# The third-last tile stored in one transfer instead of 16, and a new order for the last tile

## The chip, the cores and the metric

The kernel runs on one core of one Trainium2 chip. The metric is the device time of one execution in microseconds (us), as a median of several runs. One profiled execution of each kernel gives a trace; its span is about 1.8 us shorter than the device time of the same execution (1034.08 us against 1035.88 for the kernel before). Single executions of one kernel differ by up to 3 us. So wherever a few tenths matter I compare a piece of the trace that doesn't carry this scatter, called **the tail**: the time from the start of the last 512-column matmul (the last gate projection) to the end of the span. It is 8.38 us in the kernel before.

## The reference

Attention over spatially reduced keys and values, then a feed-forward block with a rectified gate:

```python
kv_pool = kv.reshape(B, H // r, r, W // r, r, C).mean(axis=(2, 4))
k = v = kv_pool.reshape(B, -1, C) @ w_sr
x = softmax(q @ k.T / sqrt(C)) @ v           # 49152 tokens of 128 features
out = (maximum(x @ w_gate, 0) * (x @ w_val)) @ w_out   # inner width 1536, float32 out
```

## The kernel before

The tokens are worked in 96 tiles of 512. A tile passes through stages that are software-pipelined: while tile k is attended to, tile k-3 runs its value and gate projections in 12 steps and tile k-4 its output projection. Each value/gate step writes one 128x512 block of `hT`. The output projection sums 12 blocks. It comes in two forms:

```python
def out_proj(k, fb):
    if k == NT - 2:                      # token-major: hT is the weight, 4 x 128 columns
        if fb == 0:
            o_banks[k] = bank([128, NS, 128])
        for s in range(NS):
            out_add(k, fb, s, o_banks[k][:, s, :], fb == 0 and s == 0)
        return
    if fb == 0:                          # feature-major: one matmul of 512 columns
        o_banks[k] = bank([128, T])
    nc.tensor.matmul(o_banks[k], wo16[:, fb, :], hTs[k][:, fb, :], ...)

def out_turn(k):                         # after a feature-major tile
    nc.vector.transpose(o_t, o_banks.pop(k))
    nc.gpsimd.tensor_scalar(o_sb..., o_t..., 1.0 / X_SCALE**2, None, op0=ALU.mult)
    ...                                  # in the first and last group of 4 tiles: 16 pieces of 16 KB
    return moves

def out_last(k):                         # tile 95: slices 0 and 1, then 2, then 3
    o_ps = bank([128, 2, 128])
    for s in range(2):
        for fb in range(NFB - 1):
            out_add(k, fb, s, o_ps[:, s], fb == 0 and s == 0)
    for s in range(2):
        out_add(k, NFB - 1, s, o_ps[:, s], False)
    out_scale(k, nc.vector, slice(0, 2), o_ps)
    out_store(k, slice(0, 2))
    for s in range(2, NS):
        o_ps = bank([128, 1, 128])
        for fb in range(NFB):
            out_add(k, fb, s, o_ps[:, 0], fb == 0)
        out_scale(k, (nc.scalar, nc.vector)[s % 2], slice(s, s + 1), o_ps)
    out_store(k, slice(2, NS))
...
# in the loop over stages: out_moves are issued two a step, in steps 2 to 9 of the next stage
    if step == NFB - 1 and k < last:
        out_moves = out_turn(kO)
    if 2 <= step < 10:
        for _ in range(2):
            if out_moves:
                nc.sync.dma_start(*out_moves.pop())
```

All stores are issued by SyncE, which works through its instructions in order. A token-major tile lies in the order of the output rows and goes out in one transfer of 128 packets of 2 KB, one from each partition.

The softmax here doesn't subtract the row's maximum and nothing guards it: scores larger than these inputs give would overflow.

## Time and profile before

| | before |
|---|---|
| device time | 1035.74 us median of 3 runs (1035.46 to 1036.62) |
| TensorE busy | 1023.5 us, 99% of the span |
| tail: last 512-column matmul at 1025.70, span's end at 1034.08 | 8.38 us |
| SyncE issuing pieces and stores, with one pause of 0.4 us at 1020.9 | 1013.2 to 1030.8 us |
| last store issued | 1030.44 us |

A line of the timeline reads: start, duration, engine, line of the kernel, operation, what it writes and reads, how many; in brackets, how long the engine sat idle before and who released it. A row "SPq" is SyncE issuing a transfer; its duration is the issuing, not the moving of data. The prediction below shows the lines that matter.

### The profile page before, as it was taken

How to read it: one execution, taken by the hardware profiler on the slowest of the kernel's cores; microseconds unless marked ns; L12 is line 12 of the kernel's file. 1: busy time of each engine (PE TensorE's matmuls, PEld its weight loads, DVE VectorE, ACT ScalarE, POOL GpSimd, SP SyncE). 2: the span in 40 equal slices, each digit the busy share in tenths (PEclk: the TensorE clock that was granted, in tenths of full speed). 3: DMA queues.
4: the chain of work that ended last, by engine and by line, in shares of the span. 5: the costliest groups of instructions: out<-in, count | busy, mean ns of one | idle time of the engine just before them, and what ended most of it. 6: DMA issues, size and time to landing. Idle time of an engine off the chain costs nothing.

```text
span 1034.1 us, 19981 instructions
## 1 busy us (share of the span) xinstructions
PE 1023.5 (99%) x6540; PEld 543.3 (53%) x6540; DVE 910.6 (88%) x1669; ACT 909.6 (88%) x1749; POOL 281.4 (27%) x288
## 2 busy tenths in 40 slices
PE   8999999999999999999999999999999999999998
PEld 5555555555555555555555555555555555555554
DVE  3888889998989898998889898989898989888897
ACT  4988899888888889888888888888898888889986
POOL 1212146521211125642212121664121211111111
PEclk9999999999999999999999999999999999999999
DMA  8936396562543547736345157573652533513122
GB/s 292 133 57 74 84 198 144 83 92 43 82 67 50 80 120 161 169 53 89 55 64 88 31 86 151 142 161 57 82 78 42 78 60 56 86 31 67 31 46 48
DMA packets 330840, 93.34 MB, mean 90 GB/s; under 512 B 310768, under 2 KB 324080, under 8 KB 330736
## 3 DMA queue, kind: packets, MB, share of 16 engines
q1 hardware_dynamic: 315648, 78.76, 39.1%
q0 software_dynamic: 14944, 13.24, 10.6%
q8 instruction: 51, 0.84, 0.3%
q14 instruction: 53, 0.43, 0.2%
q10 hardware_dynamic: 144, 0.07, 0.0%
HBM read 53.94 MB, written 26.35 MB: 78 GB/s over the span
## 4 chain that ended last, share of the span: by engine, by line
PE 97%; DMA 2%; DVE 0%; SPq 0%; ACT 0%; issue 0%
PE bank_ps L278 24%; PE bank_ps L289 24%; PE bank_ps L313 24%; PE bank_ps L240 12%; PE bank_ps L229 12%; DMA parts<-in_kv_dram 1%; DMA q<-in_q_dram 1%; PE bank_ps L299 0%; PE bank_ps L188 0%; DVE hT L292 0%; SPq L138 0%; ACT aT L230 0%; PE bank_ps L162 0%; PE bank_ps L180 0%; SPq L100 0%
## 5 line engine op out<-in xcount | busy, mean ns | idle before, releaser
L292 DVE SCALAR_TENSOR_TENSOR hT<-bank_ps,val 128x512 f16<-128x512 f32 x1152 | 758.2, 686 | 91.6 <-ACT val L282 71.1
L282 ACT CAST val<-bank_ps 128x512 f16<-128x512 f32 x1152 | 678.7, 591 | 102.4 <-PE bank_ps L278 100.5
L278 PE MATMUL bank_ps<-xT,wv 128*128 128x512 f16 x1152 | 436.6, 379 | 0.1
L289 PE MATMUL bank_ps<-xT,wg 128*128 128x512 f16 x1152 | 436.6, 379 | 0.0
L313 PE MATMUL bank_ps<-hT,wo 128*128 128x512 f16 x1128 | 427.5, 379 | 0.0
L230 ACT ACTIVATE aT<-bank_ps 128x512 f16<-128x512 f32 x576 | 346.3, 605 | 0.9 <-PE bank_ps L229 0.8
L323 POOL TENSOR_SCALAR o_sb<-o_t 128x512 f32<-128x512 f32 x94 | 140.0, 1489 | 700.8 <-DVE rinv L248 673.3
L240 PEld LDWEIGHTS <-aT 128*128 128x128 f16 x2304 | 177.2, 98 | 133.4 <-issue 0.9
L240 PE MATMUL bank_ps<-kv,aT 128*128 128x129 f16 x2304 | 223.5, 220 | 0.5 <-DVE kv L198 0.4
L229 PE MATMUL bank_ps<-qT,kv 128*128 128x512 f16 x576 | 216.8, 379 | 0.4 <-DVE qT L121 0.2
L278 PEld LDWEIGHTS <-wv 128*128 128x128 f16 x1152 | 112.7, 98 | 133.6 <-issue 0.2
L289 PEld LDWEIGHTS <-wg 128*128 128x128 f16 x1152 | 112.7, 98 | 68.6 <-issue 0.2
L313 PEld LDWEIGHTS <-wo 128*128 128x128 f16 x1128 | 110.4, 98 | 67.2
L229 PEld LDWEIGHTS <-kv 128*128 128x128 f16 x576 | 56.1, 98 | 68.0 <-ACT kv L182 0.8
L256 DVE TENSOR_TENSOR x<-bank_ps,rinv 128x256 f16<-128x256 f32 x188 | 79.7, 425 | 6.6
L321 DVE STREAM_TRANSPOSE o_t<-bank_ps 128x512 f32<-128x512 f32 x94 | 66.4, 706 | 0.0
L85 POOL DMA_DIRECT2D q<-in_q_dram x88 | 48.4, 557 | 0.3 <-issue 0.3
L147 POOL TENSOR_TENSOR s<-parts 128x512 f32<-128x512 f32 x36 | 44.9, 1266 | 0.0
L248 DVE RECIPROCAL rinv<-bank_ps 128x2 f32<-128x2 f32 x192 | 28.0, 146 | 0.6 <-PE bank_ps L240 0.6
L149 POOL TENSOR_TENSOR s<-s 128x512 f32<-128x512 f32 x18 | 22.8, 1269 | 1.4
L151 POOL TENSOR_TENSOR c<-s 128x256 f32<-128x256 f32 x18 | 13.1, 728 | 1.4
L173 ACT COPY kvT<-bank_ps 128x128 f32<-128x128 f32 x4 | 1.1, 266 | 11.2 <-PE bank_ps L162 9.7
(53 smaller groups left out, 94.4 us busy)
## 6 DMA issues: line engine op xcount, KB each, us to landing
parts<-in_kv_dram SPq DMA_DIRECT2D x48, 512.0 KB, 6.6
out_dram<-o_sb SPq DMA_DIRECT2D x352, 64.0 KB, 2.2
q<-in_q_dram POOLq DMA_DIRECT2D x88, 128.0 KB, 4.4
out_dram<-o_sb SPq DMA_DIRECT2D x96, 16.0 KB, 1.5
xT<-x SPq DMA_TRANSPOSE x94, 2.4
placed<-blocks SPq DMA_DIRECT2D x9, 128.0 KB, 1.8
kvT<-placed SPq DMA_DIRECT2D x36, 32.0 KB, 1.9
q<-in_q_dram SPq DMA_DIRECT2D x2, 512.0 KB, 8.3
```

The costliest lines, as they stand in the source:

```text
L85: nc.gpsimd.dma_start(q16[32 * j : 32 * (j + 1)].rearrange("t (i s) c -> t i s c", i=GRP), rows[j])
L229: nc.tensor.matmul(s_ps, kv16[:, k // NST, jc, 0:C], qT_of(k), start=True, stop=True)
L230: nc.scalar.activation(aTs[k][:, jc, :], s_ps, AF.Exp, scale=qk_scale)
L240: nc.tensor.matmul(x_ps[:, i, :], aTs[k][:, jc, s * 128 : (s + 1) * 128], kv16[:, k // NST, jc, C : 2 * C + 1], start=(jc == 0 and i == 0) ...
L256: nc.vector.tensor_tensor(x16s[k][:, 2 * half : 2 * half + 2, :], x_ps[:, :, 0:C], rinv.to_broadcast([128, 2, C]), op=ALU.mult,)
L278: nc.tensor.matmul(va_ps, wv16[:, fb * 128 : (fb + 1) * 128], xTs[k], start=True, stop=True)
L282: nc.scalar.copy(val, va_ps)
L289: nc.tensor.matmul(g_ps, wg16[:, fb * 128 : (fb + 1) * 128], xTs[k], start=True, stop=True)
L292: nc.vector.scalar_tensor_tensor(hTs[k][:, fb, :], g_ps, 0.0, vals.pop((k, fb)), op0=ALU.max, op1=ALU.mult)
L313: nc.tensor.matmul(o_banks[k], wo16[:, fb, :], hTs[k][:, fb, :], start=fb == 0, stop=fb == NFB - 1)
L321: nc.vector.transpose(o_t, o_banks.pop(k))
L323: nc.gpsimd.tensor_scalar(o_sb.rearrange("t j s c -> t s j c"), o_t.rearrange("t (s j c) -> t s j c", s=NS, j=4), 1.0 / X_SCALE**2, None, ...
```

## The change

The intent is to shorten the end of the kernel. Tile 93 becomes token-major with one store, like tile 94. In tile 95 the third slice is woven between the first two and their last block, to cover a wait for that block, and the last two slices get a store each. A changed condition in the load of q has no effect, since that function is never called for group 0.

```diff
     def out_proj(k, fb):
-        if k == NT - 2:
+        if k >= NT - 3:
...
     def out_last(k):
+        parts = [bank([128, 2, 128]), bank([128, 1, 128]), bank([128, 1, 128])]
+        owns = [slice(0, 2), slice(2, 3), slice(3, 4)]
...
+        held = NFB - 1
+        add(0, 0, held)          # add(slice, first block, end)
+        add(1, 0, held)
+        add(2, 0, held - 4)
+        add(0, held, NFB)
+        add(1, held, NFB)
+        keep(0, nc.vector)       # scale and store this part
+        add(2, held - 4, NFB)
+        keep(1, nc.scalar)
+        add(3, 0, NFB)
+        keep(2, nc.vector)
...
-                if step == NFB - 1 and k < last:
+                if step == NFB - 1 and kO < NT - 3:
                     out_moves = out_turn(kO)
+                elif step == NFB - 1 and k < last:
+                    out_scale(kO, nc.vector, slice(0, NS))
+                    out_store(kO, slice(0, NS))
```

More of the change, by code (lines that the diff above doesn't have):

```diff
@@ L79, in q_load @@
         rows = q[b, n0 : n0 + GRP * T, :]
-        if g in (0, NG - 1):
+        if g == NG - 1:
             nc.gpsimd.dma_start(q16, rows.rearrange("(p s) c -> p s c", p=128))
@@ L361, in out_last, with add, keep @@
     def out_last(k):
+        parts = [bank([128, 2, 128]), bank([128, 1, 128]), bank([128, 1, 128])]
+        owns = [slice(0, 2), slice(2, 3), slice(3, 4)]
         o_banks[k] = None
-        o_ps = bank([128, 2, 128])
-        for s in range(2):
-            for fb in range(NFB - 1):
-                out_add(k, fb, s, o_ps[:, s], fb == 0 and s == 0)
-        for s in range(2):
-            out_add(k, NFB - 1, s, o_ps[:, s], False)
-        out_scale(k, nc.vector, slice(0, 2), o_ps)
-        out_store(k, slice(0, 2))
-        for s in range(2, NS):
-            o_ps = bank([128, 1, 128])
-            for fb in range(NFB):
-                out_add(k, fb, s, o_ps[:, 0], fb == 0)
-            out_scale(k, (nc.scalar, nc.vector)[s % 2], slice(s, s + 1), o_ps)
-        out_store(k, slice(2, NS))
+        def add(s, fb0, fb1):
+            n = max(s - 1, 0)
+            for fb in range(fb0, fb1):
+                out_add(k, fb, s, parts[n][:, s - owns[n].start], fb == 0 and s != 1)
+        def keep(n, engine):
+            out_scale(k, engine, owns[n], parts[n])
+            out_store(k, owns[n])
+        held = NFB - 1
[9 more added lines that the diff above has]
+        keep(2, nc.vector)
     ctx.enter_context(tc.manual_schedule())
```

## The prediction

> **What bounds the kernel now.** The page's first part says that TensorE is the bound over the whole span:
>
> ```profile
> PE 1023.5 (99%) x6540; PEld 543.3 (53%) x6540; DVE 910.6 (88%) x1669; ACT 909.6 (88%) x1749; POOL 281.4 (27%) x288
> ```
>
> The change touches only the last three of 96 tiles, so this share decides little; the last 25 us do. Second view: the SyncE queue in the timeline, in windows that cut it finely. The columns are start, duration, engine, line, operation, tiles and count.
>
> ```profile
> 1013.81 8.23 SPq L535 DMA_DIRECT2D out_dram<-o_sb  x17
> 1021.61 7.78 SPq L535 DMA_DIRECT2D out_dram<-o_sb  x15
> ...
> 1028.96 0.43 SPq L535 DMA_DIRECT2D out_dram<-o_sb  x1
> 1029.49 0.38 SPq L352 DMA_DIRECT2D out_dram<-o_sb  x1
> 1029.96 0.38 SPq L352 DMA_DIRECT2D out_dram<-o_sb  x1
> 1030.44 0.40 SPq L352 DMA_DIRECT2D out_dram<-o_sb  x1
> ```
>
> L535 issues the pieces that the transposed tiles are stored in: tiles 92 and 93 lie in the last group, where a tile has 16 pieces of 16 KB. L352 is the store of the token-major tiles: 256 KB for tile 94, then 128 KB twice for tile 95. The queue never rests from 1013.2 to 1030.8 us; the pieces go out about every 7.78/15 = 0.52 us, the big stores every 0.47 us. So a transfer costs the queue about half a microsecond whether it carries 16 KB or 256 KB, and the tail stands behind a backlog. Third view: the timeline of the computing engines at the end, to see when the stores could have gone.
>
> ```profile
> 1025.92 0.72 PE L299 MATMUL bank_ps<-wo,hT 128*128 128x128 f16 x10
> 1026.39 0.60 ACT L347 ACTIVATE o_sb<-bank_ps 128x512 f32<-128x512 f32 x1
> 1026.86 2.30 PE L299 MATMUL bank_ps<-wo,hT 128*128 128x128 f16 x38 [0.21 <-DVE hT L292]
> 1027.91 0.42 DVE L349 TENSOR_SCALAR o_sb<-bank_ps 128x256 f32<-128x256 f32 x1 [0.51 <-PE bank_ps L299]
> 1028.57 0.28 ACT L347 ACTIVATE o_sb<-bank_ps 128x128 f32<-128x128 f32 x1 [1.58 <-PE bank_ps L299]
> 1029.19 0.29 DVE L349 TENSOR_SCALAR o_sb<-bank_ps 128x128 f32<-128x128 f32 x1 [0.86 <-PE bank_ps L299]
> ```
>
> Tile 94 is scaled at 1026.99 but its store is issued at 1029.49: 2.5 us lost to the backlog. The first half of tile 95 is ready at 1028.33 and goes at 1029.96. The last slice is ready at 1029.48 and goes at 1030.44. The landing is slow too, because all 0.5 MB moves at once. In the DMA view of 1029.4 to 1035, a digit is 0.14 us:
>
> ```profile
> DMA  5202501899999999950000000000000000000000
> out_dram<-o_sb SPq DMA_DIRECT2D x1, 256.0 KB, 2.4
> out_dram<-o_sb SPq DMA_DIRECT2D x2, 128.0 KB, 2.5
> ```
>
> The 16 DMA engines are full from 1030.4 to 1031.9. The last store lands about 2.4 us after its issue, at 1030.44 + 2.4 = 1032.8; the span ends at 1034.08, so 1.25 us follow the last landing, which the change doesn't touch. Last, the chain of waits of 1022 to 1035: VectorE carries it before the last matmuls.
>
> ```profile
> 1023.46 0.24 PE bank_ps L299 x4
> ...
> 1025.53 1.28 DVE hT L292 x2
> 1026.81 0.04 issue
> 1026.86 2.31 PE bank_ps L299 x38
> ```
>
> **What the Trainium skill says.** "Perfetto Trace Analysis", section "What 'DMA-bound' means", names as one kind a sequencer track solid with DMA slices, which are descriptor generation and not data movement. The trace agrees: in 1013 to 1029.4 SyncE is solid while the data engines show mostly 2 or 3 tenths busy. "DMA: Bandwidth & Descriptors", "Anatomy of one DMA", gives about 2.0 us fixed per DMA, most of it the write receipt of the target memory. It is fitted to GpSimd's path; here from SyncE a 16 KB piece lands in 1.5 us and the 128 KB `placed` stores in 1.8 us (page, part 6), so I use these. "TensorE: Matmul & The Clock Gate", "Back-to-back issue gap", gives about 81 ns per 128-column matmul in a stream with weight loads, and about 56 isolated. The trace decides: 38 matmuls in 2.30 us with one of 0.22 us is (2.30 - 0.22)/37 = 56 ns, weight loads included. "VectorE: DVE Perf Modes", "Why PSUM operands drop a tier", caps fp32 from PSUM at one element a cycle; the trace agrees: 425 ns for 256 elements and 292 for 128 is 133 ns per 128.
>
> **The change part by part.** The edited condition in the load of q does nothing: group 0 is never loaded by that function. Nothing before the stage of tile 93's projection changes.
>
> 1. *Tile 93 token-major, TensorE.* 12 matmuls of 512 columns become 48 of 128. The same replacement stands in the trace: three groups a step take 0.648 us where all are wide (1014.17 to 1017.41 is five steps of 3.24/5), and 0.655 in tile 94's stage (1018.06 to 1018.72, and so on). So +0.007 x 12 = +0.09 us of TensorE. It is not on the path: VectorE runs there without a gap from 1011.8 to 1027.4 (0.6 us apiece) behind TensorE, and the last input of its last hT is ready at 1026.49 for a start at 1026.71, so 0.22 us of slack remain.
>
> 2. *Tile 93's evacuation.* Off go a transpose of 706 ns on VectorE, a GpSimd scaling of 1489 ns and 16 issues of SyncE. On comes a VectorE scaling of 128x512: my estimate from the two sizes above is 425 + 2 x 133 = 691 ns, 15 ns less, in the same place of VectorE's queue. So the time at which TensorE may take up its 38 matmuls (1026.86) stays, within 0.05. GpSimd's work was hidden.
>
> 3. *SyncE.* Tile 92's 16 pieces still occupy it to 1021.6, then one store for tile 93, then it is idle: 15 issues of 0.52 us, 7.8 us, are gone. Tile 94's store goes at about 1027.1 as soon as it is scaled and has landed by 1029.5.
>
> 4. *The weave.* TensorE's wait of 0.21 us comes after only 10 of tile 95's matmuls, so it is for the eleventh hT piece (block 10) of the first slice. The new order still takes slice 0's blocks 0 to 10 first, so the wait stays. The twelfth piece, which the weave is meant to cover, is ready at 1027.40; before, it was wanted at 1026.86 + 12 x 0.056 = 1027.53, so nothing waited there. TensorE's end stays near 1029.2. The weave only delays the first half: its last matmul is number 21 of the 38 instead of number 14, 7 x 0.056 = 0.39 us later. VectorE starts it at 1028.30 and ends at 1028.72.
>
> 5. *Own stores.* Ready times are 1028.72, 1028.85 (slice 2 on ScalarE, unchanged) and 1029.48. Issues follow at 0.47 us each: 1028.74, 1029.21, 1029.68. The last is thus held 0.2 us by the two before it, and goes 0.76 us earlier than 1030.44. It carries 64 KB into engines that hold little else; between 1.5 us (16 KB) and 1.8 us (128 KB) I take 1.7, so 0.7 less than the 2.4 of now. It lands at 1031.4, and 1.25 us after that the span ends near 1032.6.
>
> Sum: -0.76 (issue) - 0.70 (landing) + 0.0 (TensorE, VectorE) = -1.46 us, rounded to 1.4 for the chance of a small wait. 1035.74 - 1.4 = 1034.3.
>
> **Rivals.** (a) *Only the issue gain counts*: the landing stays 2.4 us because a store to HBM has a floor. For it: landings of 2.2 us for the 64 KB pieces of the earlier tiles. Against it: those move 512 packets of 128 B, and 128 KB in 128 packets lands in 1.8. Then 1035.0. (b) *TensorE pays 81 ns a matmul* for tile 93, +(4 x 81 - 216) x 12 = +1.3 us; part of it would exceed the 0.22 us of slack, and the result would be near 1035.4. Tile 94's stage speaks against it. (c) *The weave is what gains*: if the wait on hT fell away, another 0.21 us, 1034.1. The count of 10 speaks against it. (d) *A bank wait takes its place*: three PSUM banks are asked for before the tile's first matmul. If the second were still held by an hT piece or tile 94's scaling, TensorE would wait; both end by 1027.4 and it is first written at about 1027.5, so at most some tenths: 1034.7. (e) *The backlog is only symptom*, something else ends the kernel: no change, 1035.7. Against it stand the 2.5 us between tile 94's scaling and its issue.
>
> **Range and chances.** Every rival lies within 1.5 us of the present time, while 2% is 20.7 us, so "same" is all but certain. The three runs of before spread from 1035.46 to 1036.62, so noise is as large as the mechanism's doubt. I take 1033.5 to 1035.3.
>
> **What would show it.** In the changed profile: SyncE with a gap from about 1022 to 1027 and tile 94's issue near 1027.1; TensorE's last group ending within 0.15 us of 1029.2, with its wait on hT still after 10 matmuls; the first half scaled at about 1028.3; the last issue at 1029.5 to 1029.8 with a landing of 1.6 to 1.9 us; no GpSimd scaling and no VectorE transpose for tile 93, and a 128x512 scaling near 690 ns. It is wrong if TensorE's end moves later by over 0.3 us, if the last landing still takes 2.4 us, or if the last issue isn't earlier.

## The result, and the profile after

The changed kernel took 1034.28 us (median of 6 runs, 1034.01 to 1035.11); the kernel before took 1036.08 us over its 6 runs (1035.46 to 1036.62). Ratios and their intervals here are not quite the ratios of these medians. The ratio is 0.9984 with a 95% interval of 0.9971 to 0.9997: faster by 0.16%, clear of equality, far inside 2%. The span fell from 1034.08 to 1032.48 us, the tail from 8.38 to 6.75. The rows from which the tail is counted, before and after:

```profile
1025.70 0.38 PE L289 MATMUL bank_ps<-xT,wg 128*128 128x512 f16 x1
1025.73 0.38 PE L290 MATMUL bank_ps<-xT,wg 128*128 128x512 f16 x1
```

In the timeline of the changed kernel (its lines are numbered one higher), SyncE now reads so, cut in windows:

```profile
1013.16 8.41 SPq L548 DMA_DIRECT2D out_dram<-o_sb  x16
1021.67 0.38 SPq L353 DMA_DIRECT2D out_dram<-o_sb  x1
...
1027.04 0.35 SPq L353 DMA_DIRECT2D out_dram<-o_sb  x1
1028.68 0.33 SPq L353 DMA_DIRECT2D out_dram<-o_sb  x1
1029.11 0.38 SPq L353 DMA_DIRECT2D out_dram<-o_sb  x1
1029.59 0.40 SPq L353 DMA_DIRECT2D out_dram<-o_sb  x1
```

The first row is tile 92's 16 pieces, the second tile 93's single store. Then SyncE rests for five microseconds, and tile 94's store goes as soon as it is scaled. The computing engines over the same stretch:

```profile
1018.88 0.68 DVE L350 TENSOR_SCALAR o_sb<-bank_ps 128x512 f32<-128x512 f32 x1
...
1025.95 3.14 PE L300 MATMUL bank_ps<-wo,hT 128*128 128x128 f16 x48
1026.41 0.60 ACT L348 ACTIVATE o_sb<-bank_ps 128x512 f32<-128x512 f32 x1
...
1028.23 0.42 DVE L350 TENSOR_SCALAR o_sb<-bank_ps 128x256 f32<-128x256 f32 x1 [0.90 <-PE bank_ps L300]
1028.50 0.28 ACT L348 ACTIVATE o_sb<-bank_ps 128x128 f32<-128x128 f32 x1 [1.48 <-PE bank_ps L300]
1029.12 0.29 DVE L350 TENSOR_SCALAR o_sb<-bank_ps 128x128 f32<-128x128 f32 x1 [0.47 <-PE bank_ps L300]
```

Tile 93's scaling on VectorE takes the place of its transpose. TensorE's last 48 matmuls end at 1029.09 (1029.16 before). They are merged in one row because their pause is short, but the pause is still there: the chain of waits names VectorE's hT before the same 38 matmuls.

```profile
1026.05 0.69 DVE hT L293
1026.74 0.05 issue
1026.79 2.31 PE bank_ps L300 x38
```

The weight loads of these 38 show the pause, before and after:

```profile
1026.85 2.12 PEld L299 LDWEIGHTS <-hT 128*128 128x128 f16 x38 [0.39 <-DVE hT L292]
1026.79 2.12 PEld L300 LDWEIGHTS <-hT 128*128 128x128 f16 x38 [0.29 <-DVE hT L293]
```

It is 0.1 us shorter, and this is the flaw of the tail. From the last wide matmul to the 38 it was 1.16 us before and is 1.06 now. (Over all profiles here it is 1.14 to 1.16 us in the four with tile 93 transposed, 1.04 to 1.06 in the seven others that have this pause.) With tile 93 token-major, TensorE gets to its last wide matmul about 0.1 us later, while VectorE, for which it then waits, does not. So 0.1 us of a shorter tail is its later start and no gain. Counted from the start of the 38 matmuls, the end came 1.53 us sooner (7.22 to 5.69 us), not 1.63.

In the DMA view of 1029.4 to 1035 (0.14 us a digit) the data engines are full for one digit at a time at most, and what was left to move is done by 1030.9:

```profile
DMA  1897492185000000000000000000000000000000
```

The view of the last window alone gives the last store's landing, 1.7 us against about 2.4 before:

```profile
out_dram<-o_sb SPq DMA_DIRECT2D x1, 64.0 KB, 1.7
```

So the last store is issued 3.86 us after the last wide matmul begins instead of 4.74, 0.88 us sooner. Of that 0.88 us, 0.1 us is the later start. The other 0.75 us of the 1.63 us of shorter tail came after the issue.

### The profile page after: what moved, and what is told of

It is laid out like the page before. It is cut to its first block, busy times and chain, and to the rows that moved or that the text cites. A ratio compares the mean times of both kernels' runs of the same rounds, so it can differ in the third digit from the quotient of the medians. Undisturbed runs are those within 1.5% of the kernel's fastest.

```text
span 1032.5 us, 20034 instructions
## 1 busy us (share of the span) xinstructions
PE 1024.0 (99%) x6576; PEld 545.4 (53%) x6576; DVE 910.6 (88%) x1669; ACT 909.2 (88%) x1749; POOL 279.5 (27%) x287
## 4 chain that ended last, share of the span: by engine, by line
PE 97%; DMA 2%; DVE 0%; SPq 0%; ACT 0%; issue 0%
PE bank_ps L279 24%; PE bank_ps L290 24%; PE bank_ps L314 23%; PE bank_ps L241 12%; PE bank_ps L230 12%; DMA parts<-in_kv_dram 1%; DMA q<-in_q_dram 1%; PE bank_ps L300 1%; PE bank_ps L189 0%; DVE hT L293 0%; SPq L139 0%; ACT aT L231 0%; PE bank_ps L163 0%; PE bank_ps L181 0%; SPq L101 0%
## 5 line engine op out<-in xcount | busy, mean ns | idle before, releaser
L314 PE MATMUL bank_ps<-hT,wo 128*128 128x512 f16 x1116 | 423.0, 379 | 0.0
L300 PEld LDWEIGHTS <-hT 128*128 128x128 f16 x144 | 10.2, 98 | 6.1 <-DVE hT L293 0.3
```

## The experiments

**Theory.** SyncE's queue held tile 94's and 95's stores back behind the 16 pieces of tile 93. Freeing it is the whole gain, through an earlier issue and through a landing that no longer shares the data engines with half a megabyte. The weave and the own stores give nothing or take a little. (For the own stores this did not hold; see e3.)

**Rivals.** The gain comes from tile 93's layout as such (no VectorE transpose, no GpSimd scaling); or the weave and the own stores bring a share of it.

All twelve runs gave correct results. In the time columns each kernel stands beside the kernel before of its own call. Tails are from one profile each; the changed kernel's repeated as 6.73 and the two-blocks kernel's as 6.45, so I take differences of 0.1 us as readable when the rows of the trace agree with them.

| run | time | before | ratio (95%) | tail |
|---|---|---|---|---|
| before | 1036.08 | | | 8.38 |
| changed kernel | 1034.28 | 1036.08 | 0.9984 (0.9971 to 0.9997) | 6.75 |
| e1 tile 93 alone | 1034.63 | 1036.21 | 0.9982 (0.9970 to 0.9995) | 6.85 |
| e2 last tile alone | 1035.79 | 1036.21 | 0.9993 (0.9980 to 1.0007) | 8.97 |
| e3 without the weave | 1033.94 | 1036.21 | 0.9976 (0.9963 to 0.9988) | 6.52 |
| e4 stores from ScalarE | 1034.71 | 1036.21 | 0.9986 (0.9973 to 0.9998) | 7.89 |
| e5 two blocks held back | 1033.97 | 1036.24 | 0.9978 (0.9965 to 0.9990) | 6.44 |
| e6 16 column pieces | 1036.08 | 1036.24 | 0.9997 (0.9983 to 1.0010) | 8.19 |
| e7 16 row pieces | 1034.29 | 1036.24 | 0.9980 (0.9967 to 0.9992) | 6.82 |
| e8 four tiles | 1034.12 | 1036.58 | 0.9983 (0.9970 to 0.9997) | 6.59 |
| e9 half the pieces from GpSimd | 1036.38 | 1036.24 | 1.0002 (0.9989 to 1.0014) | 9.41 |
| e10 e5, a store from ScalarE | 1034.23 | 1036.58 | 0.9976 (0.9963 to 0.9988) | 6.35 |
| changed kernel again | 1034.14 | 1036.02 | 0.9981 (0.9968 to 0.9993) | 6.73 |
| e5 again | 1034.16 | 1036.02 | 0.9980 (0.9966 to 0.9993) | 6.45 |

### e1: tile 93 alone

```diff
-        if k == NT - 2:
+        if k >= NT - 3:              # and the loop's scale-and-store; out_last as before
```

> The kernel before, with only tile 93 made token-major and stored at once; tile 95's order and its two stores stay as before. Theory (the backlog of SyncE is the whole gain): tile 94's store issued at 1027.0 to 1027.1, the first half of tile 95 near 1028.35, the last 128 KB near 1029.5 and landing in 1.8 to 2.0 us; profiled span about 1032.6, i.e. 1.3 to 1.6 us under the kernel before and within 0.2 us of the changed kernel. Rival (the weave and the own stores carry a share of the gain): span at 1033.0 or more.

```profile
1026.80 2.76 SPq L352 DMA_DIRECT2D out_dram<-o_sb  x3
out_dram<-o_sb SPq DMA_DIRECT2D x1, 128.0 KB, 1.9
```

The stores went at 1026.80, 1028.05 and 1029.23 and the last landed in 1.9 us. The tail is 6.85 us: 1.53 of the 1.63 us came from this part alone, 0.1 us of them the later start. The rival that gives the last tile's new order as a whole a large share falls. The last store is of 128 KB here, as before, so its size plays no part: from its issue to the end of the span it took 3.11 us instead of 3.64. So 0.53 of the 0.75 us after the issue came with the freer data engines.

### e2: the last tile alone

The new `out_last`, everything else as before.

> The kernel before, with only tile 95's new order and own stores; tile 93 still transposed and stored in 16 pieces. Theory: SyncE is busy to 1029.4, then four stores at 0.47 us each, the last issued near 1030.9 instead of 1030.4; its 64 KB land in 1.9 to 2.1 us since the engines are still full; span 1034.0 to 1034.4, so no gain, rather 0.1 us worse. Rival (weave and own stores gain by themselves): span 1033.6 or less.

SyncE was busy with the pieces until 1030.3 and the four stores followed one after another:

```profile
1013.57 16.73 SPq L544 DMA_DIRECT2D out_dram<-o_sb  x32
1030.40 1.86 SPq L352 DMA_DIRECT2D out_dram<-o_sb  x4
```

There was no gain, as the theory says; a fourth store behind a backlog only lengthens it. The tail is 0.59 us longer than before, more than the 0.1 us expected. Here two of tile 93's issues took 1.31 and 0.81 us instead of 0.43. The kernel before has one such long issue there, of 1.07 us. In sum the long issues of e2 held SyncE 0.62 us longer, which accounts for the 0.59 us of this execution.

### e3: without the weave

```diff
         add(0, 0, held)
         add(1, 0, held)
-        add(2, 0, held - 4)
         add(0, held, NFB)
         add(1, held, NFB)
         keep(0, nc.vector)
-        add(2, held - 4, NFB)
+        add(2, 0, NFB)
```

> The changed kernel without the weave: tile 95's third slice wholly after its first two, own stores kept. Theory: the first half is scaled near 1027.9 instead of 1028.2, its store goes near 1028.35, the last store isn't held any more and goes near 1029.45 instead of 1029.59; TensorE's end is unchanged; span 0.05 to 0.2 us under the changed kernel's 1032.5. Rival (the weave covers a wait on the twelfth hT piece): TensorE's last group becomes longer and the span rises by 0.1 us or more.

TensorE's group of 48 took 3.13 us, as with the weave, so the weave covers no wait. The first half was scaled 2.10 us after the last wide matmul began instead of 2.50, and the last store was issued after 3.70 us instead of 3.86. The tail is 0.23 us shorter than the changed kernel's, so the weave costs that much. The span, 1031.79, came out 0.7 us under the changed kernel's instead of the expected 0.05 to 0.2; 0.46 us of that is a start of the tail that happened to be early.

Beside e1 this run says more. Tile 93 and TensorE's order are the same in both; only the own stores differ, so that the last one carries 64 KB instead of 128.

```profile
out_dram<-o_sb SPq DMA_DIRECT2D x1, 64.0 KB, 1.7
```

The tail is 6.52 us against e1's 6.85. The last store was issued at nearly the same point (3.70 against 3.74 us after the last wide matmul), and from there to the end it took 2.82 us against 3.11. So with SyncE free the own stores gain about 0.3 us, against the theory, and the weave takes most of it back; behind the backlog (e2) they gained nothing. This rests on one profile of each; the times (1033.94 against 1034.63 us) point the same way.

### e4: the stores of tiles 94 and 95 from ScalarE

```diff
     def out_store(k, own):
-        nc.sync.dma_start(
+        nc.scalar.dma_start(
```

> The kernel before with nothing changed but the queue that issues the stores of tiles 94 and 95: ScalarE instead of SyncE. Tile 93 stays transposed, with its GpSimd scaling and its 16 pieces on SyncE. Theory (the place in SyncE's queue is what costs): tile 94's store goes near 1027.1, the first half near 1028.4, the last near 1029.6, landing in 1.9 to 2.1 us; span 1032.6 to 1032.9, nearly the whole gain without any change of layout. Rival (the gain comes from tile 93's layout, from fewer packets or from GpSimd's and VectorE's saved work): span stays near 1034.1.

This missed. Tile 94's store went at 1027.03, as expected, but the first half's went only at 1029.32 and the last at 1030.30. ScalarE shows why:

```profile
1029.99 0.28 ACT L347 ACTIVATE o_sb<-bank_ps 128x128 f32<-128x128 f32 x1 [3.12 <-DMA out_dram<-o_sb]
```

Its wait is for a transfer. In the instruction records, the semaphore that each transfer reports on is taken in turn from eight (100, 102, 104 to 107, 109 and 110), and before ScalarE issues the first half's store it waits (until just before 1029.32) on number 100, the same that this store then uses. The users of these eight just before were tile 93's pieces, which SyncE was still issuing; the one on number 100 was issued at 1026.65 and had landed at 1029.24. So the other queue didn't escape the backlog: it waited for it through the shared completion semaphores, and ScalarE's next scaling waited too. The tail is 7.89 us, a third of the gain. Part of this is the execution's: two of SyncE's pieces took 1.79 and 0.85 us and delayed the rest. The timed runs (1034.71 against 1036.21 us) show more gain, but scatter too much to tell a third of it from all. The run doesn't decide between the theory and its rival; what it adds is this wait.

### e6: tile 93 token-major, but in 16 pieces

```diff
-                    out_store(kO, slice(0, NS))
+                    out_moves = [
+                        (to[:, s, 32 * c : 32 * c + 32], o_sbs[kO][:, s, 32 * c : 32 * c + 32])
+                        for s in range(NS) for c in range(4)
+                    ]
```

> The changed kernel with tile 93 still token-major and scaled by VectorE, but stored in 16 pieces of 16 KB (128 rows of 32 columns, 128 packets of 128 B each, as the old pieces have), issued where the old ones were. Theory (the count of issues on SyncE is the cost): SyncE is busy to about 1029 us again, the last store is issued near 1030.9, tail 8.2 to 9.0 us. Rival (the gain came from the layout, the saved transpose or GpSimd's saved work): tail 6.7 to 6.9.

```profile
1022.70 6.68 SPq L556 DMA_DIRECT2D out_dram<-o_sb  x14
...
1029.95 1.84 SPq L353 DMA_DIRECT2D out_dram<-o_sb  x4
```

The new layout, the saved transpose and the saved GpSimd work are all still there, and the gain is gone: 1036.08 us beside 1036.24 for the kernel before, tail 8.19 (a hair under the lower edge of what was expected; 0.1 us of the 0.19 under the kernel before is the later start). This decides against the layout as such. The cost is the issuing.

### e7: 16 pieces of 8 rows

The pieces are `to[8 * p : 8 * p + 8]` for 16 values of p, so 8 packets of 2 KB each instead of 128 of 128 B.

> As the run with column pieces, but the 16 pieces are 8 partitions of 2 KB each: 8 packets apiece instead of 128. Theory A (an issue costs SyncE about 0.45 us whatever it carries): tail 8.0 to 9.0 us as with the column pieces. Theory B (SyncE pays per packet it describes): the pieces go out in well under 0.2 us each, SyncE is free before 1027 and the tail is 6.7 to 7.0.

```profile
1021.99 4.69 SPq L555 DMA_DIRECT2D out_dram<-o_sb  x14
...
1026.78 2.62 SPq L353 DMA_DIRECT2D out_dram<-o_sb  x4
```

Neither theory was right about the price of an issue. One of these took 0.29 us (4.69/14 = 0.34 us from one to the next) against 0.43 us for a piece of 128 packets (6.68/14 = 0.48). So an issue of 8 packets still costs two thirds of one of 128. How much of the 0.14 us between them is due to the count of packets isn't shown: the token-major stores, of 128 packets of 0.5 to 2 KB, took 0.33 to 0.41 us in these runs. It was enough: the pieces were out at 1026.68, 0.3 us after tile 94 was scaled (1026.40) but long before the next part was (1028.04), and the tail is 6.82 us, within 0.1 of the single store. Together with e6 this gives the condition: what counts in this kernel is whether SyncE is free by about 1027, not how many transfers there were.

### e9: every second piece from GpSimd

```diff
-                for _ in range(2):
+                for turn in range(2):
                     if out_moves:
-                        nc.sync.dma_start(*out_moves.pop())
+                        queue = nc.gpsimd if k == last and turn == 1 else nc.sync
+                        queue.dma_start(*out_moves.pop())
```

> The kernel before with tile 93 transposed, scaled by GpSimd and stored in 16 pieces as before, but every second piece is issued by GpSimd, and tile 95 is untouched. SyncE then has 8 pieces of 0.5 us and is free by about 1026, before tile 94's store is ready. Theory (place in SyncE's queue): stores near 1027.0, 1028.3 and 1029.5, tail 6.8 to 7.1 us, nearly the whole gain without the new layout. Rival (layout, packets or engines' work): tail 8.2 or more.

The stores did what was expected: with layout and engines' work as before, they went from 1026.89 on, three of them within 2.86 us, and the 128 KB ones landed in 1.9 us:

```profile
1026.89 2.86 SPq L352 DMA_DIRECT2D out_dram<-o_sb  x3
```

All had landed by about 1031.3, but the span went on to 1035.0. At the kernel's exit each engine drains, and GpSimd's drain, in the records of the exit line, took its time:

```profile
L618 POOLq DRAIN  x3: 46/102/9589, 1024.6 to 1034.7; - x3
```

The three numbers are the shortest, the median and the longest in ns. The longest one ran from 1024.6 to 1034.2 and ended about 8.4 us after GpSimd's last issue (1025.8). In the kernel before it took 9302 ns from 1019.7, ended at 1029.0 and bound nothing; in the changed kernel it took 9298 ns from 1011.3. So the end moved from the stores to GpSimd. The expected tail missed; the expected issue times, on which the theory rests, held.

### e8: tile 92 as well

> The changed kernel with tile 92 token-major and stored at once too. Theory: SyncE was already idle from 1022 to 1027, so freeing it from 1013 to 1021.6 as well gains nothing; tail (from the start of the last 512-column matmul to the end of the span) 6.6 to 6.9 us, as the 6.75 of the changed kernel. Rival (each transposed tile near the end costs something of its own): tail under 6.5.

The edit is `NT - 4` for `NT - 3` in both places. The tail is 6.59 us, just under the expected range and 0.16 under the changed kernel's; the last store was issued 0.07 us sooner after the last wide matmul. The time shows no gain (1034.12 us). Most of the theory stands; where the 0.16 us come from I leave open.

### e5, e10 and the repeats: a weave that covers the wait

TensorE's one wait is for block 10, so two blocks must be held back, not one:

```diff
-        held = NFB - 1
+        held = NFB - 2
...
-        add(2, 0, held - 4)
+        add(2, 0, held - 3)
...
-        add(2, held - 4, NFB)
+        add(2, held - 3, NFB)
```

> The changed kernel with two blocks of tile 95 held back instead of one (the first two slices take blocks 0 to 9, then seven blocks of the third slice, then blocks 10 and 11). Measure, as the start of the tail shifts from run to run: the tail, from the start of the last 512-column matmul to the end of the span; 8.38 us before, 6.75 in the changed kernel. Theory (TensorE's only wait is for block 10): the group of 48 takes 2.85 to 2.95 us instead of 3.13 and the tail is 6.4 to 6.6 us. Rival (the wait is of another kind, or the next one takes its place): the group stays at 3.1 us and the tail at 6.7 to 6.8.

```profile
1025.93 2.84 PE L300 MATMUL bank_ps<-wo,hT 128*128 128x128 f16 x48
```

The group of 48 took 2.84 us instead of 3.14, so TensorE's wait in the changed kernel was 0.3 us and is gone, and the tail fell to 6.44. e10 then lets ScalarE issue the third slice's store (`nc.scalar` for that part).

> The kernel with two blocks held back (tail 6.44 us), and the store of the third slice issued from ScalarE, which has just scaled it, so that the last store isn't held by it on SyncE. No pieces of tile 93 are in flight, so the completion semaphores are free. Theory: the last store goes when its slice is ready, near 1029.15 instead of 1029.3 (0.15 to 0.2 us earlier); tail 6.2 to 6.35 us. Rival (ScalarE's store brings a wait of its own, or a later end of its queue): tail 6.4 or more.

The last store was issued 3.41 us after the last wide matmul began instead of e5's 3.56, and the tail is 6.35 us, at the upper edge of the expectation. With no pieces in flight ScalarE's store met no semaphore wait, unlike in e4.

> The changed kernel itself once more, to see how well a tail measured in one profile repeats. If the tails of single profiles can be compared to about 0.1 us, it is 6.65 to 6.85 us again; the four-tile run's 6.59 against 6.75 suggests a scatter of up to 0.2 us.

> The kernel with two blocks held back once more, on the same chip and in the same rounds as the changed kernel. If removing TensorE's wait is a real gain, its group of 48 takes 2.84 us again and its tail lies 0.2 to 0.4 us under the changed kernel's of this call; if 6.44 was scatter, the tails overlap. In the timed runs 0.3 us is within the noise either way.

The tails repeated to 0.02 us: 6.73 and 6.45. So two blocks held back are a real gain of 0.3 us in the trace. In the timed runs it doesn't show: 1034.16 against 1034.14 us. The versions e3, e5 and e10 have shorter ends than the changed kernel, and no timed run can tell them from it.

## Why the prediction was right

The predicted time of 1034.3 us met 1034.28. By its own steps:

- **Step 1, TensorE in tile 93's stage.** The start of the last wide matmul is at 1025.73 against 1025.70, while VectorE in the changed kernel was 0.07 us early even before the change could act (1010.56 against 1010.63). So the stage cost about the 0.09 us predicted, and it stayed off the path; it only moved the start of the tail.
- **Step 2, the evacuation.** The 128x512 scaling took 681 ns; 691 was predicted. The 38 matmuls began at 1026.79 instead of 1026.86.
- **Step 3, SyncE.** Tile 93's store at 1021.67, then idle, then tile 94's at 1027.04: predicted 1021.6 and 1027.1. The first of the two is luck: in the kernel before, tile 92's last piece was out at 1020.86 and 1021.61 is the start of tile 93's second; in the changed kernel one issue of 1.19 us held tile 92's last piece until 1021.57. Nor did the queue quite "never rest": it waited 0.3 us for GpSimd before tile 93's first piece. e6 shows that the issuing is the cost, e7 that shorter issues suffice. The 0.52 us apiece of the working was a mean over 15 issues with one long one of 1.07 us in it; the rest follow each other every 0.475 us.
- **Step 4, the weave.** The wait stayed where it was, on block 10, as the count of 10 matmuls said; e3 shows that the weave gains nothing and e5 that holding two blocks does. The size was misread: the wait was about 0.4 us in the kernel before and 0.3 in the changed one (the weight loads' 0.39 and 0.29), not the 0.21 that the idle time before the matmuls gives, since the end of a matmul in the trace is modelled.
- **Step 5, own stores and landing.** Issues at 1028.68, 1029.11 and 1029.59 (predicted 1028.74, 1029.21, 1029.68), landing in 1.7 us as predicted. By e1 and e3, about 0.5 us after the issue came with the freer data engines and 0.2 to 0.3 with the smaller last store; the working took them as one sum.

The sum was -1.46 us, of which I kept 1.4. The tail fell by 1.63, of which 0.1 us is its later start; without that the end came 1.53 us sooner. The sum's terms were thus met within 0.05 us each: about 0.78 us in the issue (predicted 0.76) and 0.75 in what follows it (predicted 0.70). The difference of the medians, 1.80 us, includes scatter: the kernel before itself moved from 1035.74 in the first three runs to 1036.08 in six, so the exact hit of the time owes something to luck. The rivals: (a) falls with the landing of 1.7 us; (b) with the 0.09 us of step 1; (c) with e3, though its 0.21 us were to be had in another way (e5); (d) with TensorE's unchanged end; (e) with e1 and e6. No rival said that the weave itself costs: the change would have had a tail 0.23 us shorter without it (e3). Steps 4 and 5 had most of this, a first half 0.39 us later and a last store held 0.2 us by the two before it. No 2% was ever in reach.

## What to carry to other kernels

At the end of a kernel, ask not only when the last data is ready but when the queue that issues its store comes free: 16 small transfers at 0.475 us each ahead of it cost about 1.4 us here (e1) that no engine's busy time shows. Count the matmuls before a wait to see which input it is for before reordering work to cover it. Moving transfers to another queue can bring back the same wait through shared completion semaphores, or a long drain of the other engine.

## What the Trainium skill lacked or had wrong

- "DMA: Bandwidth & Descriptors", section "Issuing engines are not separate DMA queues", says that the time to initiate a DMA is usually small relative to the DMA. Here it was 0.43 us of SyncE for a piece of 128 packets (one every 0.475 us), beside a landing of 1.5 us, and 0.29 us for one of 8 packets; 16 in a row held up everything behind them. I found no Trainium2 price of an issue by packet count on the page.
- The same section says that issuing from several engines saves the sequencer's time. e4 shows a limit that it doesn't name: a store from ScalarE waited until 1029.3 us for the completion semaphore of one of SyncE's transfers, since this kernel takes them in turn from eight.
- "TensorE: Matmul & The Clock Gate", section "Back-to-back issue gap": 81 ns per 128-column matmul in a stream with weight loads; measured 56 ns over 38 in a row.
- "VectorE: DVE Perf Modes", section "The DRAIN you can't avoid", tells of drains at the start and end of a kernel, on all engines, of a constant 12 ns or so. At the exit line of this kernel GpSimd has another: it took 9302 and 9589 ns and ended about 8 us after GpSimd's last work (1021.2 to 1029.0; 1025.8 to 1034.2), which set the end of e9.
- None of the pages named in this document tells of SyncE's single long issues: in the last 13 us one of 1.07 to 1.79 us in every profile but e8's, and a second one of 0.81 and 0.85 us in e2 and e4. The traces show what lies beside them: each of the first kind coincides with a 16 KB packet of the DMA queue of kind "instruction" (before: the packet at 1024.25 for 0.88 us, the issue at 1024.46; changed kernel: 1020.29 and 1020.38; e4: 1024.29 for 1.45 us, and 1024.35), each of the second with one of 8 KB (e2: 1028.17, e4: 1027.70), though beside the 8 KB packets of before and e6 the issues took only 0.49 and 0.50 us. In e8 the 16 KB packet came at 1015.77, when SyncE issued nothing. That SyncE waits there for its own instructions would explain it, but no run tests it.
